# Weight conversions in batch 0: the point from which blocks 6 to 17 may be issued

## The chip, the cores and the metric

The kernel runs on one core of a Trainium2 chip. The metric is the device time of one execution, in microseconds (us); less is better. The core has five engines that run their own instruction streams and wait for each other by semaphores: TensorE (PE: matmuls, with PEld for its weight loads), VectorE (DVE), ScalarE (ACT), GpSimd (POOL) and SyncE (SP), which here only issues DMAs.

## The reference

Attention with a causal window of 128 keys and a slope per head, then a bilinear feed-forward layer over all 8 x 576 = 4608 tokens:

```
scores = q @ k.T / sqrt(64) + slope[h] * -|i - j|     # 8 batches, 8 heads, 576 tokens, 64 wide
attn   = softmax(where(0 <= i - j < 128, scores, -1e9))
x      = (attn @ v), heads side by side               # [4608, 512]
out    = ((x @ w_a) * (x @ w_b)) @ w_out              # 512 -> 1536 -> 512
```

All of it is float32.

## The kernel before, in words

**Tiling.** The attention goes by batch and by pair of heads: four pairs (p = 0 to 3) per batch. The feed-forward layer goes by batch, over 12 blocks of 128 hidden columns (f = 0 to 11) and two halves of 288 tokens (t). The products of the feed-forward layer are made from float16 pairs: x and the weights are each split into a high and a low half, and three matmuls of half by half make one product.

**Weights.** They come as 64-bit words, and `convert(n)` makes a float32 block of them on VectorE in three instructions over 128x1024 values: L136, L138 and L139. Blocks 0 to 11 hold w_a and w_b of one f each, blocks 12 to 17 two f of w_out each. The raw words lie in three slots (`raws[n % 3]`, in the profile wdn), the results in nine (`forms`, in the profile wsum). When L139 of block n has read its slot, SP issues the load of block n + 3 (`load_raw`, L124). Blocks 0 to 11 then go through squares on ScalarE (L145), column norms on PE (`wn_ps`, L161), a maximum on VectorE (L166, `wtop`), a scale on POOL, and the split on ScalarE (L153) and VectorE (L154) into `wup`. Blocks 12 to 17 are split at L239 and L240 into `wdn`, after a common ratio is known.

**Batch 0's attention.** `first_attention` runs the 16 score groups of batch 0: scores on PE, bias and minimum on VectorE (L595), exponentials on ScalarE, transposes on PE. `pv(p)` makes a pair's output: the reciprocal of the sums (L618, L619), its spread over partitions on PE (`rin_ps`, L625) with a copy by ScalarE (L629), the product with v on PE (`x_ps`, L515), and L636 on VectorE, which multiplies and writes x in two pieces of 512 and 64 columns; x takes the place of v. x is squared (L439) for the hidden scale `g` (norms `n_ps` L530, L531 to L537) and split into `xs`, high on ScalarE (L449), low on VectorE (L450). `last_exp[0]` is the last score operation of L595 issued so far.

**The first feed-forward batch.** `first_up` makes for each f and each half of the tokens two banks of twelve matmuls (`up_ps`, L864), one for w_a (m=0) and one for w_b (m=1). The first six matmuls of a bank use the first pairs' xs, the last six that of pairs 2 and 3. `keep` frees a bank: ScalarE copies m=0 (L800), VectorE multiplies m=1 into it (L802, needs g). L856 and L857 then make h, and `first_down` multiplies it with `wdn` (`dn_ps`, L826). Beside it run the scores of the next batch (`sc_ps` L388, L396, L397, L410 to L414).

**Order.** In this part of the program only SP's order is written out by hand. The order on the other engines is made by the framework's scheduler when the kernel is built, from dependences and its own estimates; `tc.issue_after(i)` tells it that an instruction may be placed only after instruction i. From batch 1 on PE's order is by hand too. PSUM banks come from small pools and go to whoever asks next, so a bank's new owner waits for the operation that frees it, and which one that is depends on the order.

Of the kernel before, what the change touches and what calls it, by code (L numbers as in the profile page):

```python
# [18 lines left out]
ALU = mybir.AluOpType  # L19
# [27 lines left out]
def attention_then_bilinear_ffn(ctx: ExitStack, tc: tile.TileContext, qT, kT, vP, w_a, w_b, w_out, rel, slopes2, outT):  # L47
    nc = tc.nc
    vec, act, pe, pool, sp = nc.vector, nc.scalar, nc.tensor, nc.gpsimd, nc.sync
# [76 lines left out]
    def words(n):  # L126

        w = raws[n % 3].bitcast(I32).rearrange("p m (n two) -> p m n two", two=2)
        return w[:, :, :, 0], w[:, :, :, 1], forms[n % len(forms)].bitcast(I32)

    def convert(n):

        low, high, t = words(n)

        with tc.issue_after(last_exp[0].ins) if n >= 5 else ExitStack():
            vec.tensor_scalar(out=t, in0=high, scalar1=3, scalar2=0x3FFFFFF8, op0=ALU.logical_shift_left, op1=ALU.bitwise_and)  # L136
        yield
        vec.scalar_tensor_tensor(out=t, in0=high, scalar=-0x40000000, in1=t, op0=ALU.bitwise_and, op1=ALU.bitwise_or)  # L138
        vec.scalar_tensor_tensor(out=t.bitcast(U32), in0=low.bitcast(U32), scalar=29, in1=t.bitcast(U32), op0=ALU.logical_shift_right, op1=ALU.bitwise_or)  # L139
        yield  # L140
# [36 lines left out]
    def up_weights():  # L177
# [4 lines left out]
        for f in range(NF + 2):  # L182
            conv = convert(f) if f < NF else iter(())
            next(conv, None)
            n = f - 1
            if 0 <= n < NF:
                if n % 2 == 0:
                    ps = ps_at.tile([P, 512], F32, tag="at", name="wn_ps")
                up_norms(n, sq.pop(n), ps)
            yield  # L190
            next(conv, None)
            if f < NF:
                load_raw(f + 3)
            if rest:
                rest.pop(0)()
            if 0 <= n < NF and n % 2:
                up_scales(n // 2, ps)
                hi += [(k, m) for k in (n - 1, n) for m in range(2)]
            yield
            if hi:  # L200
                rest.append(split_up(*hi.pop(0)))
            yield
            if f < NF:
                sq[f] = squares(f)
            if hi:
                rest.append(split_up(*hi.pop(0)))
            if rest:
                rest.pop(0)()
            yield
# [3 lines left out]
    def down_weights():  # L213

        sums = small.tile([P, NF // 2], F32, tag="wos", name="wos", bufs=1)
        for n in range(NF // 2 + 1):
            conv = convert(NF + n) if n < NF // 2 else iter(())
            next(conv, None)
            yield
            next(conv, None)  # L220
            if n < NF // 2:
                load_raw(NF + n + 3)
            if n:
                squares(NF + n - 1, accum_out=sums[:, n - 1:n])
            yield
        sab = small.tile([P, NF], F32, tag="sab", name="sab", bufs=1)
        vec.tensor_tensor(out=sab, in0=sup[:, :, 0], in1=sup[:, :, 1], op=ALU.mult)
        vec.tensor_reduce(out=smin, in_=sab, op=ALU.min, axis=AX)
        vec.reciprocal(sab, sab)
        s1 = small.tile([P, 1], F32, tag="wo1", name="wo1", bufs=1)  # L230
        vec.tensor_reduce(out=s1, in_=sums, op=ALU.add, axis=AX)
        tot = ps_at.tile([P, 512], F32, tag="at", name="wtot")
        total(tot[:, 0:1], s1)
        power_scale(so, tot[:, 0:1], 1.01, 15)
        vec.tensor_scalar(out=ratio, in0=sab, scalar1=smin, scalar2=so, op0=ALU.mult, op1=ALU.mult)
        yield
        for f in range(NF):
            s, x = ratio[:, f:f + 1], forms[(NF + f // 2) % len(forms)][:, f % 2, :]
            act.activation(wdn[:, f, 0, :], x, AF.Copy, scale=s)  # L239
            vec.scalar_tensor_tensor(out=wdn[:, f, 1, :], in0=x, scalar=s, in1=wdn[:, f, 0, :], op0=ALU.mult, op1=ALU.subtract)  # L240
            yield
# [30 lines left out]
    class State:  # L272
        pass

    last_pv, last_exp = [None], [None]

    def load_v(b):

        st = State()
        st.v = work.tile([P, NPAIR, VCOLS], F32, tag="v", name="v")  # L280
        sp.dma_start(st.v, vP[b])
        st.xq = work.tile([P, S], BF16, tag="xq", name="xq")
        return st
# [147 lines left out]
    def square_x(p, st, x, keep=None, tag="sq"):  # L431

        if p == 0:
            act.activation(st.xq, x, AF.Square, scale=1.02)
            st.squares = [st.xq]
        elif keep:

            sq = keep.tile([P, S], BF16, tag=tag, name="sq", bufs=2 if tag == "row" else 1)
            act.activation(sq, x, AF.Square, scale=1.02)  # L439
            st.squares.append(sq)  # L440
        else:
            sq = work.tile([P, S], BF16, tag="sq", name="sq")
            act.activation(sq, x, AF.Square, scale=1.02)
            pool.tensor_tensor(out=st.xq, in0=st.xq, in1=sq, op=ALU.add)
# [59 lines left out]
    def each_pv(xp, vts, pts):  # L504

        for b in range(5):
            for rows, oc, blocks in by_keys(b):
                w = 64 * len(blocks)
                bank0, o0 = oc < 512, oc % 512
                first = oc == 0 if bank0 else b == 3  # L510
                ends = b == 3 if bank0 else b == 4
                for n, (vt, pt) in enumerate(zip(vts, pts)):
                    for h in range(2):
                        c = 512 + 64 * h if b == 4 else 64 * (4 * h + b)
                        last = pe.matmul(xp[oc // 512][64 * h:64 * h + 64, o0:o0 + w], vt[0:rows, c:c + 64], probs(pt, rows, blocks, h), start=(n == 0 and first), stop=(n == len(vts) - 1 and ends), skip_group_check=True)  # L515
        return last
# [22 lines left out]
    def first_attention(weights, rate):  # L539
# [12 lines left out]
        for p in range(NPAIR):  # L552
# [4 lines left out]
            if p == 0:  # L557
# [3 lines left out]
                st = load_v(0)  # L561
# [52 lines left out]
        def pv(p, pt):  # L614


            rin = small.tile([P, QT], F32, tag="rin", name="rin0")
            vec.tensor_scalar(out=rin, in0=sums[p], scalar1=1e-9, scalar2=None, op0=ALU.add)  # L618
            vec.reciprocal(rin, rin)  # L619
            yield  # L620
            rp = [ps_ch.tile([P, 512], F32, tag="ch", name="rin_ps") for _ in range(2)]
            for i in range(QT):
                for e in range(2):
                    r = slice(64 * e, 64 * e + 64)
                    pe.matmul(rp[i // 8][r, 64 * (i % 8):64 * (i % 8) + 64], rin[r, i:i + 1].to_broadcast([64, 64]), ident[r, r], start=True, stop=True)  # L625
            r = first.tile([P, S], F32, tag="rin0", name="rin0", bufs=1)
            x = st.v[:, p, 0:S]
            for n, (c, w) in enumerate(halves_of_x):
                act.copy(r[:, c:c + w], rp[n][:, 0:w])  # L629
            xp = [ps_ch.tile([P, 512], F32, tag="ch", name="x_ps") for _ in range(2)]  # L630
            last = each_pv(xp, (st.v[:, p, :],), (pt,))
            if p == NPAIR - 1:
                last_pv[0] = last
            yield
            for n, (c, w) in enumerate(halves_of_x):
                vec.scalar_tensor_tensor(out=x[:, c:c + w], in0=xp[n][:, 0:w], scalar=st.sv, in1=r[:, c:c + w], op0=ALU.mult, op1=ALU.mult)  # L636
            yield
            square_x(p, st, x, first if p == 2 else work, "row" if p == 1 else "sq")
            yield

        bias(0)
        n = 4 * NPAIR
        t = exponentials(0, 0, products(0, 0))
        beside = iter(())
        for k in range(n):
            p, bi = k // 4, k % 4
            ps = products((k + 1) // 4, (k + 1) % 4) if k + 1 < n else None
            if k < n - 1:
                other(0.5)
            if bi == 1 and p + 1 < NPAIR:  # L650
                bias(p + 1)
            tp = transposed(t)
            if ps:
                t = exponentials((k + 1) // 4, (k + 1) % 4, ps)
            next(beside, None)
            keep(bi, tp, pts[p % 2])
            if p == 0 and bi < 2:
                v_squares(st, (2 * bi, 2 * bi + 1))
            if p == 0 and bi == 2:
                v_scale(st)  # L660
            if bi == 3:
                beside = pv(p, pts[p % 2])
            if k < n - 1:
                other(0.5)
# [426 lines left out]
```

## Time and profile before

| | us |
|---|---|
| median of 3 runs | 989.74 |
| the runs | 990.12, 988.67, 989.74 |
| profiled execution, its time | 987.61 |
| profiled execution, its span | 985.8 |
| ScalarE busy | 635.8 (64%) |
| POOL busy | 254.9 (26%) |
| HBM read, written | 48.33 MB, 9.44 MB |

The span runs from the first to the last instruction; the time of the execution is 1.81 us longer. A timeline row has the start and the duration in us, the engine, the line of the kernel, the operation, the tiles (out<-in), the shapes and how many instructions are put together; in brackets the idle time of the engine ahead of it and what ended that. Names in the profile leave buffer numbers out, and a tile can carry the name of the first owner of its place: the raw words are wdn, the converted blocks wsum, x is v.

### The profile page before, as it was taken

The page shows a single profiled execution, that of the slowest core. Times are in us where ns is not written, and L with a number is a line of the kernel's source. Part 1 is how long each engine was busy: PE and PEld are TensorE (multiplying, and loading weights), DVE is VectorE, ACT ScalarE, POOL GpSimd, SP SyncE. Part 2 cuts the span into 40 slices and gives each one's busy share as a digit, 9 for nine tenths or more (in the row PEclk, how much of TensorE's full clock was granted, in tenths as well). Part 3 has the DMA queues.
Part 4 walks back from the last instruction along what each step waited for, and adds up shares of the span by engine and source line. Part 5 has one row for each costly group of instructions (what it writes and reads, how often), then busy time and mean ns, then how long its engine had stood idle before and what let it go on. Part 6 is the DMA issues. An engine that isn't in the chain of part 4 may idle for free.

```text
span 985.8 us, 23840 instructions
## 1 busy us (share of the span) xinstructions
PE 960.8 (97%) x9341; PEld 749.1 (76%) x9341; DVE 667.5 (68%) x1867; ACT 635.8 (64%) x1729; POOL 254.9 (26%) x308
## 2 busy tenths in 40 slices
PE   6979999999999999999999999999999999999998
PEld 5557777777777777777787777777777777877776
DVE  5899998568688657776768677757776576514520
ACT  5958788577776657776767766777667765413321
POOL 1212122043546222541225222211232022311100
PEclk9899999999999999999999999999999999999999
DMA  9337744654437233473345362373344441210001
GB/s 359 137 116 267 200 107 84 145 148 92 86 85 181 67 69 75 110 176 78 59 92 131 111 119 65 86 193 82 61 91 105 139 74 39 55 37 2 1 13 37
DMA packets 148432, 102.82 MB, mean 104 GB/s; under 512 B 120032, under 2 KB 128352, under 8 KB 147296
## 3 DMA queue, kind: packets, MB, share of 16 engines
q1 hardware_dynamic: 138816, 91.77, 38.0%
q10 hardware_dynamic: 9504, 9.54, 3.0%
q8 instruction: 73, 1.20, 0.5%
q14 instruction: 39, 0.32, 0.1%
HBM read 48.33 MB, written 9.44 MB: 59 GB/s over the span
## 4 chain that ended last, share of the span: by engine, by line
PE 76%; DVE 10%; ACT 7%; DMA 4%; issue 2%; SPq 0%; POOL 0%; ACTq 0%; DVEq 0%
PE ch L864 19%; PE dn_ps L960 18%; PE up_ps L864 14%; PE p L864 14%; PE x_ps L515 4%; PE sc_ps L392 3%; PE dn_ps L826 3%; DMA v<-in_vP 2%; DMA wdn<-in_w_b 2%; DVE phl L414 2%; DVE xs L450 1%; DVE t L396 1%; ACT t L397 1%; ACT phl L413 1%; PE sc_ps L388 1%
## 5 line engine op out<-in xcount | busy, mean ns | idle before, releaser
L864 PEld LDWEIGHTS <-wup 128*128 128x128 f16 x3072 | 296.2, 98 | 82.0 <-issue 5.8
L960 PE MATMUL dn_ps<-h,wdn 128*128 128x288 f16 x2016 | 254.4, 286 | 0.0
L960 PEld LDWEIGHTS <-wdn 128*128 128x128 f16 x2016 | 193.9, 98 | 51.9 <-issue 0.2
L864 PE MATMUL up_ps<-xs,wup 128*128 128x288 f16 x1536 | 194.8, 286 | 1.4 <-DVE v L636 1.1
L864 PEld LDWEIGHTS <-wsum 128*128 128x128 f16 x1152 | 111.7, 98 | 32.4 <-issue 2.8
L919 POOL TENSOR_TENSOR rc<-rc,row 128x288 f32<-128x288 f32 x64 | 62.3, 973 | 279.7 <-DVE row L917 262.4
L397 ACT ACTIVATE t<-t,mn 128x192 f32<-128x192 f32 (+2 forms) x252 | 107.3, 428 | 23.4 <-DVE mn L396 23.2
L414 DVE SCALAR_TENSOR_TENSOR phl<-t,rin,phl 128x192 f16<-128x192 f32 (+2 forms) x252 | 105.8, 458 | 14.4 <-ACT phl L413 14.2
L864 PE MATMUL ch<-xs,wup 128*128 128x288 f16 x768 | 115.0, 286 | 0.1
L864 PE MATMUL p<-xs,wup 128*128 128x288 f16 x768 | 115.1, 286 | 0.0
L864 PE MATMUL ch<-xs,wsum 128*128 128x288 f16 x768 | 111.5, 286 | 1.7 <-ACT rc L889 1.7
L856 ACT CAST h<-rc 128x576 f16<-128x576 f32 x96 | 64.2, 669 | 67.1 <-DVE rc L924 37.3
L413 ACT ACTIVATE phl<-t,rin 128x192 f16<-128x192 f32 (+2 forms) x252 | 88.9, 425 | 23.8 <-DVE rin L410 10.9
L857 DVE TENSOR_TENSOR h<-rc,h 128x576 f16<-128x576 f32 x90 | 69.5, 772 | 29.9 <-ACT h L856 29.1
L396 DVE CUSTOM_DVE_ANT_0 t<-sc_ps,bias,neg 128x192 f32<-128x192 f32 (+2 forms) x216 | 73.9, 389 | 7.8 <-PE sc_ps L392 7.8
L965 ACT ACTIVATE row<-dn_ps,oi 128x288 f32<-128x288 f32 x56 | 27.6, 493 | 55.6 <-PE dn_ps L960 55.5
L450 DVE TENSOR_TENSOR xs<-v,xs 128x576 f16<-128x576 f32 x52 | 48.6, 947 | 21.9 <-ACT xs L449 21.7
L901 ACT ACTIVATE row<-ch,g 128x288 f32<-128x288 f32 x64 | 31.8, 497 | 48.9 <-PE ch L864 48.9
L896 DVE TENSOR_TENSOR rc<-p,rc 128x288 f32<-128x288 f32 x64 | 29.1, 454 | 44.1 <-PE p L864 34.7
L373 POOL TENSOR_SCALAR bias<-rel_sb,ninv,sl_sb 128x192 f32<-128x192 f32 x24 | 20.0, 833 | 147.5 <-DVE mn L396 129.5
L864 PE MATMUL p<-xs,wsum 128*128 128x288 f16 x384 | 57.5, 286 | 0.0
L924 DVE SCALAR_TENSOR_TENSOR rc<-rc,g,ch 128x288 f32<-128x288 f32 x64 | 32.7, 511 | 23.6 <-PE ch L864 23.4
(155 smaller groups left out, 1376.8 us busy)
## 6 DMA issues: line engine op xcount, KB each, us to landing
v<-in_vP SPq DMA_DIRECT2D x8, 1280.0 KB, 6.4
out<-row ACTq DMA_DIRECT2D x62, 144.0 KB, 1.8
qk<-in_qT SPq DMA_DIRECT2D x28, 288.0 KB, 4.0
qk<-in_kT SPq DMA_DIRECT2D x28, 288.0 KB, 4.5
wdn<-in_w_a SPq DMA_DIRECT2D x12, 512.0 KB, 6.1
wdn<-in_w_b SPq DMA_DIRECT2D x12, 512.0 KB, 7.0
wdn<-in_w_out SPq DMA_DIRECT2D x12, 512.0 KB, 5.9
qst<-qkh SPq DMA_DIRECT2D x24, 144.0 KB, 2.9
```

The source lines that it names most:

```text
L396: vec.tensor_tensor_reduce(out=t[:, c:c + w], in0=ps[:, c:c + w], in1=o.bias[:, WIN - w:WIN], scale=-0.125 if o.b == 1 else o.neg, scalar= ...
L397: act.activation(t[:, c:c + w], t[:, c:c + w], AF.Exp, bias=o.mn[:, n:n + 1], scale=-1.0, accum_out=o.sm[:, n:n + 1])
L413: act.activation(phl[:, 0, pc:pc + w], e, AF.Copy, scale=s)
L414: vec.scalar_tensor_tensor(out=phl[:, 1, pc:pc + w], in0=e, scalar=s, in1=phl[:, 0, pc:pc + w], op0=ALU.mult, op1=ALU.subtract)
L450: vec.tensor_tensor(out=xs[:, n, 1, :, :], in0=src, in1=xs[:, n, 0, :, :], op=ALU.subtract)
L515: last = pe.matmul(xp[oc // 512][64 * h:64 * h + 64, o0:o0 + w], vt[0:rows, c:c + 64], probs(pt, rows, blocks, h), start=(n == 0 and first ...
L856: act.copy(h[:, f, :, 0, :], hid)
L857: eng.tensor_tensor(out=h[:, f, :, 1, :], in0=hid, in1=h[:, f, :, 0, :], op=ALU.subtract)
L864: pe.matmul(ps[:, 0:HT], w[:, wi, k, :], xs[:, b, xi, k, :], start=(first and n == 0), stop=(last and n == len(ks) - 1), skip_group_check= ...
L919: pool.tensor_tensor(out=x0, in0=x0, in1=mid, op=ALU.mult)
L924: vec.scalar_tensor_tensor(out=x1, in0=x1, scalar=st.g, in1=ch, op0=ALU.mult, op1=ALU.mult)
L960: pe.matmul(ps[:, 0:HT], wdn[:, f, wi, e * P:(e + 1) * P], h[:, f, t, hi, :], start=(m == 0 and n == 0), stop=(m == NF - 1 and n == 2))
```

## The change

Three lines. `kept[p]` keeps the instruction that writes the second piece of pair p's x. L136, the first operation of a conversion, was tied to the last score operation of batch 0 for all blocks from 5 on. Now block 5 is tied to that, blocks 6 and 7 to the second piece of pair 2's x, and blocks 8 to 17 to the second piece of pair 3's x. L138 and L139 follow L136 by their data.

```diff
@@ convert(n)
-        with tc.issue_after(last_exp[0].ins) if n >= 5 else ExitStack():
+        with tc.issue_after((last_exp[0] if n < 6 else kept[2] if n < 8 else kept[3]).ins) if n >= 5 else ExitStack():
             vec.tensor_scalar(out=t, in0=high, scalar1=3, scalar2=0x3FFFFFF8, op0=ALU.logical_shift_left, op1=ALU.bitwise_and)
...
-    last_pv, last_exp = [None], [None]
+    last_pv, last_exp, kept = [None], [None], {}
...
             for n, (c, w) in enumerate(halves_of_x):
-                vec.scalar_tensor_tensor(out=x[:, c:c + w], in0=xp[n][:, 0:w], scalar=st.sv, in1=r[:, c:c + w], op0=ALU.mult, op1=ALU.mult)
+                kept[p] = vec.scalar_tensor_tensor(out=x[:, c:c + w], in0=xp[n][:, 0:w], scalar=st.sv, in1=r[:, c:c + w], op0=ALU.mult, op1=ALU.mult)
```

The scheduler makes a new order from it on all engines but SP, whose order is the same. On VectorE between x of pair 1 and x of pair 2 (`x_ps_635` and `x_ps_636` are pair 2's two banks; three L136 have been issued ahead of these rows), before:

```order
L138 SCALAR_TENSOR_TENSOR wsum_121<-wdn_122,wsum_121 128x1024 x2
L618 TENSOR_SCALAR rin0_695<-sm0_562 128x9
L138 SCALAR_TENSOR_TENSOR wsum_121<-wdn_122,wsum_121 128x1024
L450 TENSOR_TENSOR xs_125<-v_148,xs_125 128x576
L139 SCALAR_TENSOR_TENSOR wsum_121<-wdn_122,wsum_121 128x1024
L450 TENSOR_TENSOR xs_125<-v_148,xs_125 128x576
L139 SCALAR_TENSOR_TENSOR wsum_121<-wdn_122,wsum_121 128x1024
L619 RECIPROCAL rin0_695<-rin0_695 128x9
L139 SCALAR_TENSOR_TENSOR wsum_121<-wdn_122,wsum_121 128x1024
L636 SCALAR_TENSOR_TENSOR v_148<-x_ps_635,sv_268,rin0_632 128x512
L636 SCALAR_TENSOR_TENSOR v_148<-x_ps_636,sv_268,rin0_632 128x64
```

The same place now, from x of pair 1 to x of pair 3 (`x_ps_721` and `x_ps_722`), with one L136 issued ahead:

```order
L138 SCALAR_TENSOR_TENSOR wsum_121<-wdn_122,wsum_121 128x1024
L618 TENSOR_SCALAR rin0_695<-sm0_562 128x9
L139 SCALAR_TENSOR_TENSOR wsum_121<-wdn_122,wsum_121 128x1024
L619 RECIPROCAL rin0_695<-rin0_695 128x9
L450 TENSOR_TENSOR xs_125<-v_148,xs_125 128x576 x2
L636 SCALAR_TENSOR_TENSOR v_148<-x_ps_635,sv_268,rin0_632 128x512
L636 SCALAR_TENSOR_TENSOR v_148<-x_ps_636,sv_268,rin0_632 128x64
L136 TENSOR_SCALAR wsum_121<-wdn_122 128x1024 x2
L138 SCALAR_TENSOR_TENSOR wsum_121<-wdn_122,wsum_121 128x1024 x2
L139 SCALAR_TENSOR_TENSOR wsum_121<-wdn_122,wsum_121 128x1024 x2
L636 SCALAR_TENSOR_TENSOR v_148<-x_ps_721,sv_268,rin0_718 128x512
L636 SCALAR_TENSOR_TENSOR v_148<-x_ps_722,sv_268,rin0_718 128x64
```

Blocks 6 and 7 went from between pair 1's and pair 2's x to between pair 2's and pair 3's, and the rest behind pair 3's. The second place is further on VectorE, where the first m=1 banks of the up projection (`up_ps_871`, `up_ps_914`, `up_ps_963`) are freed and block 10's conversion begins, before:

```order
L802 SCALAR_TENSOR_TENSOR rc_821<-rc_821,g_758,up_ps_871 128x288
L802 SCALAR_TENSOR_TENSOR rc_821<-rc_821,g_758,up_ps_914 128x288
L406 TENSOR_SCALAR rin_846<-sm_845 128x5
L802 SCALAR_TENSOR_TENSOR rc_931<-rc_931,g_758,up_ps_963 128x288
L410 RECIPROCAL rin_846<-rin_846 128x5
L154 SCALAR_TENSOR_TENSOR wup_120<-wsum_121,sup_126,wup_120 128x2x256 x4
L136 TENSOR_SCALAR wsum_121<-wdn_122 128x1024
L138 SCALAR_TENSOR_TENSOR wsum_121<-wdn_122,wsum_121 128x1024
```

And now (the L294 converts sums of the squares of v that ScalarE makes):

```order
L537 TENSOR_SCALAR g_758<-x2e_756 128x1
L294 CAST vc16_1247<-vs_1073 128x4
L136 TENSOR_SCALAR wsum_121<-wdn_122 128x1024
L802 SCALAR_TENSOR_TENSOR rc_821<-rc_821,g_758,up_ps_871 128x288
L802 SCALAR_TENSOR_TENSOR rc_821<-rc_821,g_758,up_ps_914 128x288
L802 SCALAR_TENSOR_TENSOR rc_931<-rc_931,g_758,up_ps_963 128x288
L406 TENSOR_SCALAR rin_846<-sm_845 128x5
L138 SCALAR_TENSOR_TENSOR wsum_121<-wdn_122,wsum_121 128x1024
```

Block 10's L136, which reads the raw words of its DMA, and L294 stand ahead of the three L802 now; L136 stood behind them.

## The prediction

> **What bounds the kernel now.** I read the page first: who is busy, and at which clock.
>
> ```profile
> PE 960.8 (97%) x9341; PEld 749.1 (76%) x9341; DVE 667.5 (68%) x1867; ACT 635.8 (64%) x1729; POOL 254.9 (26%) x308
> PE   6979999999999999999999999999999999999998
> PEclk9899999999999999999999999999999999999999
> ```
>
> PE (TensorE) is busy 97% of the span, and slices of 24.6 us below 9 stand only at the start. So time can be won only where PE waits or runs at a lower clock, and an edit to VectorE's order matters as far as it shifts PE's waits. The edit acts from 48.8 us on, behind batch 0's last score operation. So next I read the timeline of PE from there (start, duration, line, operation, tiles; in brackets the idle time ahead and what ended it).
>
> ```profile
> 54.17 1.97 PE L515 MATMUL x_ps<-phl,v 128*64 128x128 f32 x28
> 56.07 2.01 PE L864 MATMUL up_ps<-xs,wup 128*128 128x288 f16 x15
> 60.55 1.26 PE L625 MATMUL rin_ps<-ident,rin 64*64 64x64 f32 x36 [2.46 <-DVE v L636]
> 62.44 3.63 PE L515 MATMUL x_ps<-pT,v 128*64 128x128 f32 x28 [0.27 <-ACT rin L629]
> 65.99 1.05 PE L161 MATMUL wn_ps<-wsq,ones 128*128 128x256 bf16 x8
> 67.67 0.90 PE L864 MATMUL up_ps<-xs,wup 128*128 128x288 f16 x6 [0.63 <-DVE v L636]
> 68.99 1.26 PE L864 MATMUL up_ps<-xs,wup 128*128 128x288 f16 x9 [0.43 <-DVE v L636]
> 70.19 0.88 PE L388 MATMUL sc_ps<-qkl,qkh 64*64 64x64 f32 x12
> 71.25 2.25 PE L864 MATMUL up_ps<-xs,wup 128*128 128x288 f16 x17
> ```
>
> Three of the four idle times are put down to L636 on VectorE (DVE), the multiplication that makes a pair's x out of x_ps: 2.46 us for the third pair (p=2), 0.63 and 0.43 us for the last (p=3). The fourth loss is no idle time: the same 28 matmuls of x_ps take 1.97 us at 54.17 and 3.63 us at 62.44. The clock in stretches of 2 us says why (columns: PE busy with instructions in brackets, granted clock, DMA share, GB/s).
>
> ```profile
> 62.00:64.00 2.00, 1.73 (x14) 0.61 0.97 373
> 64.00:66.00 2.00, 2.00 (x19) 0.53 0.55 217
> 66.00:68.00 2.00, 1.37 (x15) 1.00 0.07 29
> ```
>
> Half clock from about 62.5 to 65.9: 3.63 - 1.97 = **1.66 us** lost. Why x comes late shows in VectorE's timeline.
>
> ```profile
> 48.79 1.90 DVE L136 TENSOR_SCALAR wsum<-wdn 128x1024 int32<-128x1024 int32 x3
> 50.60 0.94 DVE L636 SCALAR_TENSOR_TENSOR v<-x_ps,sv,rin 128x512 f32<-128x512 f32 x2
> 51.46 2.35 DVE L138 SCALAR_TENSOR_TENSOR wsum<-wdn,wsum 128x1024 int32<-128x1024 int32 x2
> 53.80 1.22 DVE L138 SCALAR_TENSOR_TENSOR wsum<-wdn,wsum 128x1024 int32<-128x1024 int32 x1
> 55.60 1.22 DVE L139 SCALAR_TENSOR_TENSOR wsum<-wdn,wsum 128x1024 uint32<-128x1024 uint32 x1
> 58.66 1.17 DVE L139 SCALAR_TENSOR_TENSOR wsum<-wdn,wsum 128x1024 uint32<-128x1024 uint32 x1
> 59.74 0.94 DVE L636 SCALAR_TENSOR_TENSOR v<-x_ps,sv,rin 128x512 f32<-128x512 f32 x2
> 61.94 0.69 DVE L136 TENSOR_SCALAR wsum<-wdn 128x1024 int32<-128x1024 int32 x1 [1.26 <-DMA wdn<-in_w_b]
> 66.26 0.69 DVE L136 TENSOR_SCALAR wsum<-wdn 128x1024 int32<-128x1024 int32 x1 [1.10 <-DMA wdn<-in_w_b]
> 66.87 0.75 DVE L636 SCALAR_TENSOR_TENSOR v<-x_ps,sv,rin 128x512 f32<-128x512 f32 x1
> 68.66 0.28 DVE L636 SCALAR_TENSOR_TENSOR v<-x_ps,sv,rin 128x64 f32<-128x64 f32 x1
> 70.58 0.75 DVE L450 TENSOR_TENSOR xs<-v,xs 128x576 f16<-128x576 f32 x1
> 71.88 0.76 DVE L450 TENSOR_TENSOR xs<-v,xs 128x576 f16<-128x576 f32 x1
> ```
>
> x_ps of p=2 is complete on PE at 54.17 + 1.97 = 56.14, but its L636 starts at 59.74: VectorE is in the conversions of weight blocks 5, 6 and 7 (three L136, three L138, three L139). Pair 3's L636 stands behind a wait for a weight DMA (1.10 us) and its second half behind one more L138. So these conversions, not the data, set when PE goes on.
>
> **The change part by part.** It adds and removes no instruction; it moves conversions behind x. Durations, start to start: L136 0.60 (1.81 / 3), L138 and L139 1.13 (59.74 - 58.66 = 1.08 with no successor of its kind, 2.35 for two), L636 0.86 for both halves (51.46 - 50.60), L450 0.67.
>
> - *x of p=1.* One L136 stands ahead of it in place of three: 48.79 + 0.60 = 49.39 for 50.60. PE gains 1.2 us there, which it uses for up-projection matmuls that came later.
> - *x of p=2.* Ahead of it are now L138 and L139 of block 5 alone, two short operations and the two L450 of the earlier pairs: 50.25 + 2 x 1.13 + 0.2 + 2 x 0.67 = 54.06. VectorE then waits for x_ps: PE has done ten more up matmuls first, starts x_ps at about 54.75 and ends its first bank some 1.7 later, so L636 starts at **56.45 for 59.74**. VectorE's new wait of 2.4 us takes the place of the old 1.26 + 1.10: its total idle time does not change.
> - *PE's wait of 2.46 us* (rin_ps for p=3) goes: six up matmuls reach to 57.39, x's first half is out at 57.1. rin_ps 57.39 for 60.55; x_ps 1.89 later as before (62.44 - 60.55), 59.28 for 62.44.
> - *The clock.* With no wait over 1 us on PE ahead of x_ps, I take it at 1.97 us instead of 3.63, so it ends at 61.2 for 66.07.
> - *x of p=3.* Blocks 6 and 7 stand in full between the two x: 57.31 + 2 x 0.60 + 4 x 1.13 = 63.05, both halves together, for 66.87 and 68.66. New cost: x_ps is ready at 61.2, so this wait of 1.9 us is the conversions'. PE has 0.9 us of norms (wn_ps) beside it and then idles about 1.8 us.
> - *The low halves of xs (L450)* for pairs 2 and 3: behind L636 stand one L136, one top (0.60) and one L138, so they end at about 67.0 and 67.7, for 70.58 + 0.75 = 71.33 and 72.64. PE waits here for 0.8 us more.
> - *The second halves of the first up-projection banks* need those. Before, 2 + 15 of the 17 matmuls at 71.25, so they start at 71.5; after, at 67.15: 4.35 us earlier. But the scores at 70.19 (0.81 us start to start) are not done yet then. **Lead of PE: 4.35 - 0.81 = 3.5 us**, 1.66 of it the clock.
>
> DMA issues move too. The load of raw block 9 is issued when L139 of block 6 has read its slot: 62.0 for 58.65. SP issues in order, so the first q and k of batch 1 go behind it, 62.9 to 63.7 for 59.51 to 60.4. They need 5.8 to 6.2 us to land, 69.3 at the latest, when PE wants them: cost 0 to 0.5 us, taken as 0, since 1.6 MB are under way where there were 2.6. The v of the next batches goes by the last L450:
>
> ```profile
> 72.70 0.33 SPq L281 DMA_DIRECT2D v<-in_vP  x1
> 75.14 0.43 SPq L124 DMA_DIRECT2D wdn<-in_w_b  x1
> 83.11 0.69 DVE L136 TENSOR_SCALAR wsum<-wdn 128x1024 int32<-128x1024 int32 x1 [0.32 <-DMA wdn<-in_w_b]
> 77.88 0.94 DVE L802 SCALAR_TENSOR_TENSOR rc<-rc,g,up_ps 128x288 f32<-128x288 f32 x2
> 113.67 0.50 DVE L802 SCALAR_TENSOR_TENSOR rc<-rc,g,up_ps 128x288 f32<-128x288 f32 x1
> 146.17 7.38 DVE L240 SCALAR_TENSOR_TENSOR wdn<-wsum,ratio,wdn 128x512 f16<-128x512 f32 x11 [0.24 <-ACT wdn L239]
> 156.48 6.42 PE L826 MATMUL dn_ps<-h,wdn 128*128 128x288 f16 x51
> ```
>
> Issued at 67.8 instead of 72.70, and raw block 10 at 70.5 for 75.14; it landed 8.0 us after (83.11), so now at about 78.1.
>
> **Does the lead last?** Two rows of before: all engines over one stretch (busy, instructions; PE, weight load, DVE, ACT, POOL), and the first wait of PE after it.
>
> ```profile
> 72.00:153.00 81.00, 80.86 (x748) 61.78 (x746) 78.85 (x192) 66.96 (x170) 16.09 (x16) 1.00 0.57 177
> 153.21 1.63 PE L864 MATMUL up_ps<-xs,wup 128*128 128x288 f16 x12 [0.34 <-ACT rc L800]
> ```
>
> PE runs without a wait there, so the lead is kept if VectorE and ScalarE free the banks in time; but VectorE is busy 78.85 of 81 us and can gain some 2 us at most. VectorE's own position is the same in both: at 72.5 before it has conversions up to 9 done; after, at 67.7, it still owes L136, L138 and L139 of block 9, L139 of block 8 and one score triple, 4.6 us, which makes 72.3. I walked its new order from there: the first L802 (banks 871, 914, 963) at 78.7 to 79.9, those of 1083 and 1177 at 92.5 and 93.4, 1219 at 99.4, 1421 at 110.6 (113.67 before: the new order has conversions 11 to 13 behind it). PE asks for these banks at 80.4, 94.0, 95.5, 101 and about 111. So slack is 0.4 to 2 us, and no wait follows. At the end, 33 of the 36 matmuls of the first down-projection bank (f = 0 to 10) come ahead of those for the last h; the block of L240, 146.17 before and 144 to 146 now, is done by 151.5 to 153.5, and PE starts dn_ps at about 153 (156.48 - 3.5) and needs its last row 4 us later. Cost 0 to 1.5 us; I take 0. **Sum: -3.5 us** on the profiled execution's 987.61 us, 984.1. That execution lies 2.13 us under the median of the runs, 989.74; on the median the forecast is **986.2 us**.
>
> **The rivals.** *VectorE takes the lead back.* For it: VectorE's position is unchanged, it is 97% busy (78.85 / 81), and its slack is under 2 us at several banks. Against it: the new order puts the L802 ahead of conversions. PE would wait in several places between 80 and 165 us, and of the 3.5 us only what VectorE can shed is left at the most, 2 us (81 - 78.85), at the least nothing: 987.7 to 989.7, say 989.0.
>
> *The slow clock stays.* A half-clock stretch of 3.4 us followed a wait of 2.46 us before; after, PE still idles about 1.8 and 0.8 us between 62 and 67. If the stretch falls on the dense up matmuls then, 1.66 us of the lead are lost: -3.5 + 1.66 = -1.84, 987.9. The Trainium skill bears on this ("TensorE: Matmul & The Clock Gate", Part 1: The HAM clock gate): the array drops to half clock after at least one idle window of about 3.4 us, and the window runs free. By that rule no wait here is long enough, before or after; the trace agrees with the length of 3.4 us, but the stretch came after a wait of 2.46 us, so the measurement decides and the rival keeps its chance.
>
> *VectorE stands at raw block 10: slower.* Before, the L802 of 871, 914 and 963 come ahead of block 10's L136, at 77.88 and on; after, they stand behind it. If that load lands as late as before (83.11 for 78.1), the first L802 ends at 84.2, PE waits 84.2 - 80.4 = 3.8 us at the bank of 871, which alone cancels the lead, and all of VectorE's order behind it shifts by 5 us: the L802 of 1421 at 115.6 is 1.9 us later than before. That gives +2 us, 991.7. It decides once the load lands after about 83; against it speaks that nothing on SP holds the issue back once the L450 are earlier.
>
> *That the change moves nothing* is excluded: the order of instructions has the conversions behind x.
>
> **How the numbers follow.** Forecast 986.2 (985.0 to 987.7: from one us more out of VectorE's earlier L802, to 1.5 us lost at dn_ps): 0.56. VectorE takes it back, 989.0: 0.20. Slow clock, 987.9: 0.11. Raw block 10, 991.7: 0.13. 0.2% is 1.98 us, about what a measurement can tell from no change. Faster by more (under 987.76): 0.56; within: 0.20 + 0.11 = 0.31; slower: 0.13. Range 984.4 to 990.3: the first three cases, with 0.6 us below and above for the spread of the runs (988.67 to 990.12).
>
> **What would show it.** Right: no wait of over 1 us on PE between 54 and 61; the third x_ps of 28 matmuls at about 2 us; L636 of p=2 at about 56.5 and of p=3 at 63; granted clock 1.00 from 60 to 68; dn_ps starting near 153 (156.48 before). Wrong: a wait at up_ps put down to L802 between 80 and 112 us; a half-clock stretch behind 62 us; VectorE waiting for in_w_b at 79 us or later; or dn_ps starting at 156 again.

## The result and the profile after

The changed kernel takes 994.83 us (median of 6 runs, 993.05 to 996.56) beside 989.49 us before (6 runs, 988.46 to 990.12): a ratio of 1.0052, 95% interval 1.0039 to 1.0066. It is **slower by 0.5%**, where the forecast was 0.36% faster and the range ended at 990.3. The profiled execution of after took 994.83 us, its median; that of before took 987.61 us, 1.9 us under its median of 989.49. So differences between the two traces are up to 2 us larger than those of the medians. To compare places in the two I count from the first L136 behind batch 0's last scores (48.79 us before, 50.22 after), since ahead of it the traces differ by 1.43 us, and the two VectorE orders are still the same there.

First, PE's timeline after (columns as in the prediction), from the third pair's x to the batch that follows.

```profile
59.06 1.26 PE L625 MATMUL rin_ps<-ident,rin 64*64 64x64 f32 x36
60.95 1.97 PE L515 MATMUL x_ps<-pT,v 128*64 128x128 f32 x28 [0.27 <-ACT rin L629]
65.66 2.00 PE L864 MATMUL up_ps<-xs,wup 128*128 128x288 f16 x15 [1.75 <-DVE v L636]
68.85 2.37 PE L864 MATMUL up_ps<-xs,wup 128*128 128x288 f16 x18 [0.59 <-DVE xs L450]
...
143.17 0.18 PE L106 MATMUL wtot<-c,ones 128*128 128x1 bf16 x1 [0.48 <-DVE c L105]
...
153.44 1.27 PE L826 MATMUL dn_ps<-h,wdn 128*128 128x288 f16 x9
...
167.34 1.54 PE L515 MATMUL x_ps<-pT,vhl 128*64 128x128 f16 x42 [1.56 <-DMA pT<-phl]
...
187.71 2.77 PE L515 MATMUL x_ps<-pT,vhl 128*64 128x128 f16 x42 [4.31 <-DMA pT<-phl]
```

Up to 153 us this is close to the prediction: the wait of 2.46 us is gone, the third x_ps takes 1.97 us instead of 3.63, the waits of 1.75 and 0.59 us are the predicted 1.8 and 0.8. One short wait, of 0.48 us at 143.17, was not predicted. Then come two waits that the prediction does not have, both for the DMA that transposes batch 1's probabilities (`pT<-phl`). The second, of 4.31 us, also brings the half clock back: x_ps takes 2.77 us. The same two places before:

```profile
163.18 1.54 PE L515 MATMUL x_ps<-pT,vhl 128*64 128x128 f16 x42 [0.28 <-DVE rin L406]
182.63 1.51 PE L515 MATMUL x_ps<-pT,vhl 128*64 128x128 f16 x42
```

The transpose is issued by SP (L419) as soon as the last L414 has written phl. When that was, SP's timelines of before and then of after say (start, and the time that the issue took):

```profile
156.02 5.33 SPq L419 DMA_TRANSPOSE pT<-phl  x1
171.17 5.65 SPq L419 DMA_TRANSPOSE pT<-phl  x1
```

```profile
160.59 4.84 SPq L419 DMA_TRANSPOSE pT<-phl  x1
178.67 6.57 SPq L419 DMA_TRANSPOSE pT<-phl  x1
```

With the 1.43 us taken off, the first is 3.1 us later than before and the second 6.1 us. What is late ahead of the second shows on ScalarE, which writes the high half of the last probabilities (L413), before and after:

```profile
169.16 1.49 ACT L413 ACTIVATE phl<-t,rin 128x192 f16<-128x192 f32 x4 [0.45 <-DVE rin L410]
174.54 1.16 ACT L334 ACTIVATE qkl<-qk 128x1152 bf16<-128x1152 f32 x1 [3.89 <-PE sc_ps L392]
```

```profile
175.51 1.16 ACT L334 ACTIVATE qkl<-qk 128x1152 bf16<-128x1152 f32 x1 [4.20 <-PE sc_ps L392]
...
176.68 1.48 ACT L413 ACTIVATE phl<-t,rin 128x192 f16<-128x192 f32 x4
```

The two have changed places. L334 squares the q and k of a later pair and has two things to wait for: PE's scores, which still read the tile that it writes, and the load of that k, which SP issues at 171.08 and which takes 4.3 us to land, until 175.4. With L334 ahead, ScalarE stands still for 4.20 us, and the four L413, whose L410 was done at 172.0, wait with it. No line of the diff speaks of L334: the scheduler, working on other times, has placed the two the other way round.

### The profile page after: what moved, and what is told of

Read it like the earlier page. It is cut to its first block, busy times and chain, and to the rows that moved or that the text cites. A ratio compares the mean times of both kernels' runs of the same rounds, so it can differ in the third digit from the quotient of the medians.

```text
span 993.0 us, 23847 instructions
## 1 busy us (share of the span) xinstructions
PE 964.1 (97%) x9341; PEld 750.8 (76%) x9341; DVE 667.4 (67%) x1867; ACT 635.4 (64%) x1729; POOL 253.4 (26%) x308
## 4 chain that ended last, share of the span: by engine, by line
PE 68%; DVE 12%; DMA 8%; ACT 8%; issue 2%; SPq 1%; ACTq 0%; POOL 0%; DVEq 0%
PE ch L864 19%; PE dn_ps L960 18%; PE p L864 14%; PE up_ps L864 10%; PE x_ps L515 4%; DMA v<-in_vP 3%; PE sc_ps L392 3%; DVE phl L414 2%; DMA wdn<-in_w_b 2%; PE dn_ps L826 1%; ACT t L397 1%; DVE xs L450 1%; DVE t L396 1%; DVE wsum L139 1%; DVE wsum L138 1%
## 5 line engine op out<-in xcount | busy, mean ns | idle before, releaser
L414 DVE SCALAR_TENSOR_TENSOR phl<-t,rin,phl 128x192 f16<-128x192 f32 (+2 forms) x252 | 106.6, 462 | 19.3 <-ACT phl L413 19.0
L413 ACT ACTIVATE phl<-t,rin 128x192 f16<-128x192 f32 (+2 forms) x252 | 89.0, 425 | 27.5 <-DMA pT<-phl 9.7
L864 PE MATMUL p<-xs,wsum 128*128 128x288 f16 x384 | 57.6, 286 | 0.0
L515 PE MATMUL x_ps<-pT,vhl 128*64 128x128 f16 (+2 forms) x1176 | 44.0, 232 | 5.9 <-DMA pT<-phl 5.9
```

What stands on the lines that cost most here:

```text
L413: act.activation(phl[:, 0, pc:pc + w], e, AF.Copy, scale=s)
L414: vec.scalar_tensor_tensor(out=phl[:, 1, pc:pc + w], in0=e, scalar=s, in1=phl[:, 0, pc:pc + w], op0=ALU.mult, op1=ALU.subtract)
L864: pe.matmul(ps[:, 0:HT], w[:, wi, k, :], xs[:, b, xi, k, :], start=(first and n == 0), stop=(last and n == len(ks) - 1), skip_group_check= ...
```

## The experiments

**Theory A**, formed on these rows: PE's lead came about as predicted, and two late transposes took it and more, the second by the swap of L334 and L413. **Rival B**: with the change the conversions come too late on VectorE, and the wait would show somewhere else if not there. Four kernels, then four more. Ratios are to the kernel before, with 95% intervals.

**e1: the swap undone, all else as changed.** The edit ties L334 of that pair behind the last L413 issued (the changed lines, without the one that makes `last_norm`):

```diff
-        act.activation(lo.bitcast(BF16), qk, AF.Square, accum_out=sums)
+        with tc.issue_after(last_norm[0].ins) if (b, p) == (2, 1) else ExitStack(): act.activation(lo.bitcast(BF16), qk, AF.Square, accum_out=sums)
...
-            act.activation(phl[:, 0, pc:pc + w], e, AF.Copy, scale=s)
+            last_norm[0] = act.activation(phl[:, 0, pc:pc + w], e, AF.Copy, scale=s)
```

The order differs from that of the changed kernel in two places alone: L334 and the four L413 on ScalarE, and their neighbours L337 and L414 on VectorE.

> The changed kernel with one thing put back: the four L413 (and L414) that end pair 3's probabilities of batch 1 stand ahead of the L334 of a later pair again, as before the change; every conversion stays where the change put it. Theory A (the loss is the late transpose that follows from this swap): the wait of 4.31 us on PE at x_ps and the 1.26 us at the lower clock behind it go, the wait of 1.56 us ahead of it stays: 994.8 - 5.6 = 989.2 us. Rival B (the late conversions keep VectorE behind, and the wait only shows there): PE waits as long somewhere else, 993 to 995 us.

Measured: 987.81 us, ratio 0.9984 (0.9976 to 0.9993). By the ratios that is 0.68%, 6.7 us, less than the changed kernel, and a little less than before; it is 1.4 us under theory A's number. PE's timeline at the two x_ps:

```profile
166.66 1.54 PE L515 MATMUL x_ps<-pT,vhl 128*64 128x128 f16 x42 [1.58 <-DMA pT<-phl]
...
182.55 1.51 PE L515 MATMUL x_ps<-pT,vhl 128*64 128x128 f16 x42
```

The second wait and the slow x_ps are gone, the first is as it was, and no new wait has come: B falls as the cause of the loss. L334 starts at 174.61, put down to the load of k, but the L413 that feed the transpose no longer stand behind it.

**e2: the swap alone, in the kernel before.** The squares of that pair are made one step earlier in the program, and the four L413 are tied behind them:

```diff
+        last_sq[0] = act.activation(lo.bitcast(BF16), qk, AF.Square, accum_out=sums)
...
+            with tc.issue_after(last_sq[0].ins) if (o.b, o.p) == (1, 3) and a else ExitStack(): act.activation(phl[:, 0, pc:pc + w], e, AF.Copy, scale=s)
...
-                nxt = squares(i + 1)
+                nxt = early.pop() if early else squares(i + 1)
...
+                early.extend([squares(i + 2)] if i == 3 else [])
```

No conversion moves, and on PE, POOL and SP no instruction.

> The kernel before with that swap alone: L334 ahead of the four L413, no conversion moved. Theory A: L413 waits for L334, which waits for PE's scores at 174.5; the last L414 ends at about 178, the transpose is issued then and lands 6.7 to 8.9 us later, 184.8 to 187, where PE wants it at 182.6: 2.2 to 4.4 us of waiting and 0 to 1.3 us of lower clock, 991.7 to 995.2 us. Rival B: nothing that matters is moved, 989.5 us.

Measured: 996.23 us, ratio 1.0066 (1.0053 to 1.0079). The timelines of ScalarE, PE and SP:

```profile
174.21 1.16 ACT L334 ACTIVATE qkl<-qk 128x1152 bf16<-128x1152 f32 x1 [5.71 <-DMA qk<-in_kT]
...
175.38 1.48 ACT L413 ACTIVATE phl<-t,rin 128x192 f16<-128x192 f32 x4
```

```profile
186.84 2.77 PE L515 MATMUL x_ps<-pT,vhl 128*64 128x128 f16 x42 [4.24 <-DMA pT<-phl]
189.55 4.10 PE L826 MATMUL dn_ps<-h,wdn 128*128 128x288 f16 x24
```

```profile
177.37 4.84 SPq L419 DMA_TRANSPOSE pT<-phl  x1
```

The same wait and the same slow x_ps as in the changed kernel, with no conversion moved: +6.6 us, above theory A's 2.2 to 5.7. L334 waits here for the load of k, not for the scores that A named. The transpose took 9.5 us from its issue to PE's start (186.84 - 177.37), longer than the 6.7 to 8.9 assumed, and the half clock lasts into the dn_ps behind: 4.10 us for 3.11 before. Wait, x_ps and dn_ps together are 4.24 + 1.26 + 0.99 = 6.5 us, all of the loss.

**e3 and e4: each half of the change alone.** For e3 blocks 6 and 7 are tied to pair 2's x and the rest to the last scores; for e4 blocks 8 to 17 to pair 3's x and the rest to the last scores. Neither order has the swap. Of the edits the condition alone is shown:

```diff
-(last_exp[0] if n < 6 else kept[2] if n < 8 else kept[3])
+(last_exp[0] if n < 6 or n >= 8 else kept[2])      # e3
+(last_exp[0] if n < 8 else kept[3])                # e4
```

> Half of the change: blocks 6 and 7 tied to pair 2's x, blocks 8 to 17 to the last scores as before. The swap of L334 and L413 does not come about in this order. Theory A: PE's lead up to dn_ps is kept in part and no late second transpose follows, 986.5 to 989 us. Rival B (the loss is that blocks 8 to 17 are late): faster too, 986 to 988 us; the two part at the next kernel.

> The other half: blocks 8 to 17 tied to pair 3's x, 6 and 7 to the last scores as before. The swap does not come about here either. Theory A: no wait over 2 us at the second x_ps, within 1.5 us of before, 988 to 991 us. Rival B (the loss is that blocks 8 to 17 are late): 992 to 995 us.

Measured: e3 993.43 us, ratio 1.0038 (1.0023 to 1.0053); e4 992.77 us, ratio 1.0031 (1.002 to 1.0041). For e3 both theories miss; for e4 A misses and B's number is met. The waits of PE over 1 us, e3 (the view of its first row ends at 60 us, so it shows 16 of 36 matmuls) and then e4:

```profile
59.49 0.68 PE L625 MATMUL rin_ps<-ident,rin 64*64 64x64 f32 x16 [1.75 <-DVE v L636]
67.22 3.42 PE L864 MATMUL up_ps<-xs,wup 128*128 128x288 f16 x15 [2.89 <-DVE v L636]
...
168.74 2.45 PE L515 MATMUL x_ps<-pT,vhl 128*64 128x128 f16 x42 [2.51 <-DMA pT<-phl]
```

```profile
60.36 1.99 PE L625 MATMUL rin_ps<-ident,rin 64*64 64x64 f32 x36 [2.45 <-DVE v L636]
71.13 3.22 PE L864 MATMUL up_ps<-xs,wup 128*128 128x288 f16 x25 [1.46 <-DVE xs L450]
102.30 0.60 PE L161 MATMUL wn_ps<-wsq,ones 128*128 128x256 bf16 x4 [1.46 <-ACT wsq L145]
```

With half of the change the waits for x stay: in e3 later blocks stand ahead of pair 3's x (2.89 us, and 15 matmuls in 3.42 us instead of 2.00), in e4 blocks 6 and 7 stand ahead of pair 2's (2.45 us, as before the change). So the halves win no lead, and e3 has a late first transpose as well (2.51 us, its x_ps at a lower clock). In e4 the two waits of 1.46 us are new. The one at 102 us is for the squares of a converted block (L145); they stand on ScalarE behind four L153, which waited 3.85 us for POOL's scale until 98.75, while the last L139 ahead of them was done at 97.0. Whether this goes back to late conversions, as B would have it, and whether these two waits are all that puts e4 behind the kernel before, was not tested.

**e5, e6, e7: other steps.** With L334 tied as in e1 for e5 and e6 (e7 does not have the swap):

```diff
-(last_exp[0] if n < 6 else kept[2] if n < 8 else kept[3])
+(last_exp[0] if n < 6 else kept[3])                              # e5
+(last_exp[0] if n < 6 else kept[2] if n < 7 else kept[3])        # e6
+(last_exp[0] if n < 6 else kept[2])                              # e7
```

> As e1 (four L413 ahead of L334), but blocks 6 and 7 too are tied to pair 3's x, so no conversion stands between pair 2's x and pair 3's. Theory A' (PE's lead comes from x, and its fate is set by the transpose of pair 2's probabilities, behind the block of L240): x of pair 3 comes 1.7 us earlier and PE's lead at the xs grows by as much, but VectorE idles longer ahead of it, so the conversions, the ratio and the block of L240 come some 2 us later, PE waits 3 to 4 us instead of 1.6 at the first transposed x_ps, and the end is 988.5 to 990.5 us. Rival C (what PE gains at x is kept): 986.1 us.

> As e5, but block 6 alone is tied to pair 2's x, blocks 7 to 17 to pair 3's. In its order all three conversions up to L138 still stand ahead of pair 3's x where the scheduler puts block 7 and 8 by its own estimate, if it does so, x of pair 3 is late as before. Theory A': the lead is that of e1 or less and the transpose no earlier, 988 to 991 us. Rival C: within 1 us of e1, 987 to 988.8 us.

> Blocks 6 to 17 all tied to pair 2's x. In this order three L136, three L138 and one L139 stand ahead of the first piece of pair 3's x and another L139 ahead of its second piece. Theory A': pair 2's x is early, pair 3's x comes 2 us later than in the changed kernel, so half of the lead is lost again at the xs, 989 to 992 us. Rival C': only pair 2's x counts, 987 to 988.5 us.

Measured: e5 993.65 us, ratio 1.0034 (1.002 to 1.0047); e6 **986.63 us, ratio 0.9962 (0.9947 to 0.9976)**; e7 990.39 us, ratio 1.0002 (0.9993 to 1.0012). e5 is slower than both its expectations and e6 faster than both; e7 is in the range of A'. The expectation of e6 took its order for that of e7; in e6 block 6 alone stands between the two x. VectorE's timeline of e6 at the x of pairs 2 and 3, and PE's at the transposed x_ps:

```profile
57.03 0.94 DVE L636 SCALAR_TENSOR_TENSOR v<-x_ps,sv,rin 128x512 f32<-128x512 f32 x2 [2.70 <-PE x_ps L515]
...
61.70 0.94 DVE L636 SCALAR_TENSOR_TENSOR v<-x_ps,sv,rin 128x512 f32<-128x512 f32 x2 [0.60 <-PE x_ps L515]
```

```profile
164.98 1.54 PE L515 MATMUL x_ps<-pT,vhl 128*64 128x128 f16 x42 [0.50 <-DMA pT<-phl]
180.47 1.54 PE L515 MATMUL x_ps<-pT,vhl 128*64 128x128 f16 x42 [0.41 <-DMA pT<-phl]
```

One block fills the time between the two x almost exactly (VectorE waits 0.60 us), and both transposes are nearly in time: 3.6 us less than before (990.21 in these runs), the best of all kernels here. Its order differs from e1's on several engines, so what each of these two gives was not tested. In e5, with no block between, VectorE waits 3.72 us for pair 3's x_ps, and a price comes, as A' had it, but elsewhere and larger:

```profile
61.64 0.94 DVE L636 SCALAR_TENSOR_TENSOR v<-x_ps,sv,rin 128x512 f32<-128x512 f32 x2 [3.72 <-PE x_ps L515]
```

```profile
65.71 2.00 PE L864 MATMUL up_ps<-xs,wup 128*128 128x288 f16 x15 [0.76 <-DVE xs L450]
68.64 1.39 PE L864 MATMUL up_ps<-xs,wup 128*128 128x288 f16 x10 [0.94 <-DVE xs L450]
70.91 6.04 PE L864 MATMUL up_ps<-xs,wup 128*128 128x288 f16 x48 [0.88 <-ACT rc L800]
79.47 0.88 PE L388 MATMUL sc_ps<-qkl,qkh 64*64 64x64 f32 x12 [2.52 <-DMA qkl<-in_kT]
```

What the earlier x wins is given back in short waits within 10 us, and then the first scores of batch 1 wait 2.52 us for k, which SP issues behind a load of raw words (L124) that waits for a conversion, at 73.60 us, where in e1 it is issued at 64.43:

```profile
72.28 0.33 SPq L124 DMA_DIRECT2D wdn<-in_w_a  x1
...
73.60 0.43 SPq L318 DMA_DIRECT2D qkl<-in_kT  x1
```

A' named the transpose for the loss; the trace shows this load ahead of it, and at the two transposed x_ps PE waits 0.36 and 0.71 us alone. In e7 three L138 and an L139 stand ahead of pair 3's x; PE waits 2.36 us there, and the end is that of before, as A' expected.

**e8: the first transpose earlier.** On top of e1, L308 (and L309) of pair 3's v behind both L413 of pair 2's probabilities:

```diff
-          act.activation(vhl[:, 0, :], st.v[:, p, :], AF.Copy, scale=st.sv)
+          with tc.issue_after(norms[1, 2].ins) if p == 3 and not states.get(1) else ExitStack(): act.activation(vhl[:, 0, :], st.v[:, p, :], AF.Copy, scale=st.sv)
```

> As e1, with one thing more: ScalarE's L308 (and VectorE's L309) for pair 3's v stand behind both L413 (L414) of pair 2's probabilities instead of between them. The first transpose is issued about 1.2 us earlier. In this order PE's x_ps of that pair also stands 12 matmuls (1.5 us) earlier, so the wait ahead of it stays at 1.5 to 2 us, but its x and the scores behind it come earlier. Theory A': the end gains 0 to 1.2 us on e1, 986.6 to 988.0 us. Rival: the first transpose costs nothing in the end, since the next thing behind it is as late as before, 987.8 us.

Measured: 989.37 us, ratio 0.9986 (0.9974 to 0.9998), the same as e1 within the intervals. The wait stays at 1.57 us and nothing is gained, but the edit did not bring the transpose forward either. It is issued 110.40 us behind the first L136 counted from above (158.85 - 48.45), in e1 110.45 (159.90 - 49.45): the L414 come closer behind the block of L240, but in this trace that block starts 1.3 us later than in e1's, and so does PE's dn_ps. PE waits 0.68 us at 80.22 and 0.21 us at 88.38, which it does not do in e1's trace, though the order of instructions up to there is the same. So two single traces can differ by 1.3 us where their orders agree, and what the first transpose alone is worth stays open.

## Why the prediction was wrong, step by step

*What bounds PE between 54 and 67 us: right.* With 1.43 us taken off: x of pair 2 at 56.8 (56.45 predicted), rin_ps at 57.6 (57.39), x of pair 3 at 63.4 (63.05), the second halves of the up-projection banks at 67.4 (67.15).

*The clock: right.* x_ps took 1.97 us; the granted clock was 1.00 throughout.

*The lead: right in kind, 0.7 us too large.* dn_ps starts at 153.44 - 1.43 = 152.01 for 156.48; the two groups of scores and the small sum that were done ahead of it before (156.48 - 154.77 = 1.71 us) are not done yet, so the lead is 4.47 - 1.71 = 2.76 us, not 3.5. Of the difference 0.48 us is the wait at 143.17, for the sum of the output weights' squares (L231, L105).

*The walk of VectorE over the banks: right.* PE waits at no L802. The row of after for that stretch (PE, weight load, DVE, ACT, POOL):

```profile
72.00:143.00 71.00, 70.69 (x627) 53.38 (x625) 68.88 (x164) 53.89 (x142) 12.71 (x14) 1.00 0.61 195
```

*The rival of raw block 10* did not come: VectorE waited 0.59 us for the words, until 80.20 - 1.43 = 78.77 (78.1 predicted).

```profile
80.20 0.69 DVE L136 TENSOR_SCALAR wsum<-wdn 128x1024 int32<-128x1024 int32 x1 [0.59 <-DMA wdn<-in_w_b]
```

*The step that failed* is the end of "Does the lead last?": "Cost 0 to 1.5 us; I take 0." It asked what PE needs for dn_ps, found that in time, and stopped there; the transposes that PE needs next were put at nothing. Two things stand behind it. First, the block of L240 was taken to start at 144 to 146 us and to be done by 151.5 to 153.5, and it came later:

```profile
148.81 4.73 DVE L240 SCALAR_TENSOR_TENSOR wdn<-wsum,ratio,wdn 128x512 f16<-128x512 f32 x7
154.09 4.42 DVE L240 SCALAR_TENSOR_TENSOR wdn<-wsum,ratio,wdn 128x512 f16<-128x512 f32 x5
...
160.11 0.41 DVE L414 SCALAR_TENSOR_TENSOR phl<-t,rin,phl 128x192 f16<-128x192 f32 x1
```

With the 1.43 us off it starts at 147.4 and ends at 157.1. For dn_ps that was early enough; but the last L414 of pair 2's probabilities stands behind it, at 158.7 (160.11 - 1.43) instead of some 155.5, and the transpose behind that. Ahead of the block the trace shows late conversions: the last L139 ends at 140.1 (141.55 - 1.43) for 136.95 before, ScalarE's squares wait for it, and L231, PE's sum (the wait of 0.48 us) and the ratio that L240 needs follow. So far rival B is right, for this first and smaller part; no run has it alone. Second, and by far the larger part: ScalarE's order past dn_ps was not followed at all. The swap of L334 and L413 stood in the new order already, and it makes the second transpose late: 4.31 us of waiting and 1.26 us of half clock, where the prediction has 0. Why the scheduler made it is not shown.

*The sum by these rows*, with gain below zero: lead -2.76, first transpose +1.28 (1.56 - 0.28), second +4.31, its x_ps at a lower clock +1.26 (2.77 - 1.51). That is +4.1 us. From the common point to the same scores of batch 2 the traces differ by more:

```profile
264.38 0.27 PE L392 MATMUL sc_ps<-qkh,qst 128*64 128x192 f16 x2 [0.41 <-DVE mn L396]
```

```profile
271.31 0.27 PE L392 MATMUL sc_ps<-qkh,qst 128*64 128x192 f16 x2 [0.41 <-DVE mn L396]
```

(271.31 - 50.22) - (264.38 - 48.79) = +5.5 us; the medians say +5.3. Of the remaining 1.4 us, 0.8 lie between the first dn_ps and the second transposed x_ps: the same matmuls (180 dn_ps among them) keep PE busy for 28.40 us after and 27.58 before, with no wait on record, and why is not shown. Another 0.17 is the dn_ps behind that x_ps (24 in 3.28 us for 3.11) and 0.29 a wait for ScalarE's copy L875 at 220.11; the rest, 0.2, I cannot assign. From e1 and e2 the swap's own price is 6.7 and 6.6 us, of which the wait and the slow x_ps show 5.6 in the changed kernel (4.31 + 1.26).

*The rivals.* The slower one was a mechanism at another place; that the loss could come from an order between two instructions that the diff does not touch was in none of them, and this is what the range lacked. Without the swap (e1) the kernel is 0.07 to 0.24% faster than before, where 0.36% was forecast. That fits the lead less the first transpose's wait (2.76 - 1.28 = 1.5 us, 0.15%), though in e1's own trace only 0.7 us of it is left at the second x_ps (133.10 us behind the first L136 for 133.84 before).

## What to carry to other kernels

Where a scheduler makes the order, an edit changes all that it places afterwards; compare the new order to the end of the region in which it differs, on every engine, and look for an instruction that may wait for a DMA or for another engine and has moved ahead of one that feeds a transfer. An earlier wait removed is worth only what the next fixed transfer lets through, so follow the lead to the first DMA whose landing PE needs, not to the next matmul group. And if a tie has a number in it, try its neighbours: here the same idea gave from -0.38% (one block between) to +0.52% (two, with the swap).

## What the runs showed of the hardware that was not expected

Half clock came behind waits from 2.45 us on. Granted clock behind the second transpose of after, then e1 at the same work without the wait (columns: PE busy, clock, DMA share, GB/s):

```profile
187.00:190.00 3.00, 2.29 (x33) 0.56 0.06 21
190.00:192.00 2.00, 2.00 (x28) 0.80 0.12 44
```

```profile
183.00:186.00 3.00, 3.00 (x49) 1.00 0.00 1
```

After waits of 2.45 (e4), 2.46 (before), 2.51 and 2.89 (e3), 2.52 (e5), 4.24 (e2) and 4.31 us (after) the granted clock was at 0.50 no later than 2 us after PE's next start; after 1.75 us (after) and 2.36 us (e7) it stayed at 1.00. The Trainium skill ("TensorE: Matmul & The Clock Gate", Part 1: The HAM clock gate) has the drop after at least one idle window of about 3.4 us; only the two waits over 4 us fit that. By these runs a wait of 2.45 us can be enough; whether its length alone decides was not tested.

The transpose of phl does not take the same time everywhere. Time from issue to landing of the two transposes of after, and of e1 (smallest, median, largest of the two):

```profile
DMA to landing us min/median/max: 6.7/7.8/8.9
```

```profile
DMA to landing us min/median/max: 6.7/7.1/7.5
```

The first takes 6.7 us in both; the second takes 8.9 us, issued at 178.67, and 7.5 in e1, issued at 173.39. It is not simply that a later one takes longer: before, the second is issued earlier than either, at 171.17, and takes 8.3 us; in e2 it is issued at 177.37 and takes 9.3. What makes the difference is not shown.
